# Decayed attention and a gated MLP on one core: the scores of a pair of heads from split q and k in place, on half of the array's rows each

## The chip, the core and the metric

The kernel runs on one NeuronCore of one Trainium2 chip. The core has a matrix engine (TensorE, PE in the profile, with a row of its own, PEld, for its weight loads), three engines for elementwise work (VectorE or DVE, ScalarE or ACT, GpSimd or POOL) and a queue that issues most DMAs (SyncE, SP). Each engine runs its own list of instructions in order, and semaphores make one wait for another. The metric is the device time of one execution in microseconds (us).

## The reference

For 8 batches of 8 heads, with 576 tokens and 64 dimensions per head, and then a gated MLP over the heads side by side (512 columns):

```python
scores = scale * np.matmul(q, k.transpose(0, 1, 3, 2))
log_f = np.log(np.clip(f, 0.0001, 1.0))
cum = np.cumsum(log_f, axis=-1)
decay = cum[:, :, :, None] - cum[:, :, None, :]
scores = np.where(causal, -1000000000.0, scores + decay)
...
attn = attn / (np.sum(attn, axis=-1, keepdims=True) + 1e-09)
return np.matmul(attn, v).astype(np.float32)
...
h = np.maximum(x @ w_in, 0.0)
u, v = (h[..., :d_ff // 2], h[..., d_ff // 2:])
...
v_s = np.einsum('ts,bsd->btd', w_spatial, v_n) + b_spatial[None, :, None]
gated = u * v_s
return (gated @ w_out).astype(np.float32)
```

All of it is asked for in float32.

## The kernel before, in words

**Numbers.** A float32 operand x is held as two parts: hi, x rounded to the type float32r, and lo, x minus hi. A product is hi times hi plus hi times lo plus lo times hi. `split` (L202) makes hi and lo of q and k for a pair of heads: rows 0 to 63 of the tiles hold the first head's 64 dimensions, rows 64 to 127 the second's; the columns are 640 for q (576 tokens, with a place of its own for the tail of each head) and 576 for k.

**Scores.** The heads go in 32 pairs, four pairs to a batch. A head's scores are computed in four blocks of 128 queries against 128, 256, 384 and 512 keys (`scores`, L254); the last 64 queries of both heads share one tile (`scores_tail`, L280, twice 288 keys). For each head `prep` (L215) assembles two operand tiles by DMA out of `hi` and `lo`: `ta` holds q's hi and lo stacked on 128 partitions, against k's hi twice, so that one product gives hi*hi + lo*hi; `tb` holds q's hi and the rows of the decay (68 partitions), against k's lo and the decay, so that a second product gives the rest. That makes six DMAs per head, all on SP's queue. The decay enters as four more rows of the contraction: -8 against the cumulated log decay in two parts, and the reverse. They are made once for all heads and stand in DRAM as `rows_d`. The first pair (`NQ = 1`) is an exception: one float32 tile per head, `tf`, with 66 partitions. `qkt` (L246) issues the two products of a block into one bank of PSUM, `sc`, of which there are two once the MLP runs (three before that).

A block is then masked and scaled by DVE with the row's minimum (L264), goes through exp on ACT (L266) into the tile `tt`, and is divided by its row sum by POOL (L277). `transposes` (L317) turns it on PE (against `ident`) and ACT and DVE take it out in two parts, `eh` and `el` (L314, L315); `attend` (L350) multiplies by v, into `x0` and `x1`. For the first five pairs (`NF`) that product is in float32, and its last one has the 64 keys of the tail: 64 partitions.

**MLP.** `moe` (L429) does one batch: w_in, gate statistics, the spatial product and w_out, all as three-term products into banks called `ps`.

**Order.** `attention` and `moe` are generators that yield an estimate of PE's time after each step; the loop at the end (L566) calls them alternately, so that attention runs a quarter of a batch ahead. That gives each instruction its place in the program; the framework's scheduler then sets the final order on each engine by a simulated timeline, in which an instruction whose operands or bank are not ready is passed by others. So neighbours in the code need not be neighbours on PE. With weights loaded ahead, about the first five pairs run without the MLP beside them.

Of the kernel before, what the change touches and what calls it, by code (L numbers as in the profile page):

```python
# [19 lines left out]
NF = 5            # pairs of heads whose attention times v is in float32  # L20
NQ = 1            # pairs of heads whose scores are in float32
# [17 lines left out]
def attn_gmlp_kernel(ctx: ExitStack, tc: tile.TileContext, qk, v, f, w_in, w_sp, b_sp, w_out, out):  # L39
    """Decayed causal attention, then a gated MLP with a spatial gate.  # L40

    A float32 operand x of a matrix product is held as two float32r parts, hi = x rounded to
    float32r and lo = x - hi, and a product is hi*hi + hi*lo + lo*hi, summed in float32.
    """
# [30 lines left out]
    # ---- decay rows of the score products: [-8 | c_hi], [-8 | c_lo], [c_hi | 8], [c_lo | 8],  # L75
    # the queries' columns as in qk, then the keys'; c = cumulated log decay; [-8 | c], [c | 8] in float32 ----
# [3 lines left out]
    def decay_consts(r, rows):  # L80
        r = f32(r)
        G.memset(r[:, 0:rows, 0:640], -8.0)
        G.memset(r[:, rows:2 * rows, 640:QK], 8.0)
        for p0, h in ((0, 0), (32, 1)):
            V.memset(r[p0:p0 + 32, :, S - 64 * h:640 - 64 * h], 0.0)

    def queries_rows(r, rows, copy, copy_tail):
        r_ = f32(r)
        copy(r[:, rows:2 * rows, 0:TL], r_[:, 0:rows, 640:640 + TL])
        for p0, h in ((0, 0), (32, 1)):  # L90
            copy_tail(r[p0:p0 + 32, rows:2 * rows, TL + 64 * h:S + 64 * h], r_[p0:p0 + 32, 0:rows, 640 + TL:QK])

    def decay_rows():
# [4 lines left out]
        r0 = cst.tile([64, 2, QK], F32, name="r0", tag="el")  # L98
        decay_consts(r0[:], 1)
# [3 lines left out]
        V.tensor_tensor_scan(out=r0[:, 0, 640:QK], data0=ones, data1=ft, initial=0.0, op0=ALU.mult, op1=ALU.add)  # L103
        queries_rows(r0[:], 1, V.tensor_copy, A.copy)
        return r0

    def split_rows(ws, r0):
        rt = ws.tile([64, 4, QK], F32R, name="rt", bufs=1)
        decay_consts(rt[:], 2)
        A.copy(rt[:, 0, 640:QK], r0[:, 0, 640:QK])  # L110
        G.tensor_tensor(out=rt[:, 1, 640:QK], in0=r0[:, 0, 640:QK], in1=f32(rt[:, 0, 640:QK]), op=ALU.subtract)
        queries_rows(rt[:], 2, A.copy, A.copy)
        SY.dma_start(out=rows_d[:], in_=f32(rt[:]))
# [21 lines left out]
    def load64(src, dh, dl, raw, w, a, mark=None):  # L135
        """A block of a float64 weight, read as two 32-bit words: round to float32 and split."""
# [16 lines left out]
    def load_first(ws):  # L153
        """What the first steps of the MLP need: w_in for the gate's half, the spatial weights."""
# [26 lines left out]
    def load_rest(n, w_v, dh, dl, tag, bufs):  # L181
        """An eighth of a weight, by way of tiles that the MLP doesn't use yet."""
# [17 lines left out]
    vts, tab, parts, r0s = {}, {}, {}, []  # L200

    def split(P):  # L202
        """q and k of a pair of heads, one head on each half of the partitions, split."""
        if P < NQ:
            return
        raw = wk.tile([128, QK], F32, name="raw", tag="raw")
        SY.dma_start(out=raw, in_=qk[P])
# [3 lines left out]
        for c in (slice(0, 640), slice(640, QK)):  # L211
            G.tensor_tensor(out=lo[:, c], in0=raw[:, c], in1=f32(hi[:, c]), op=ALU.subtract)  # L212
        parts[P] = (f32(hi[:]), f32(lo[:]))

    def prep(P, h):  # L215
        """The operands of a head's scores: ta = [q_hi; q_lo | k_hi; k_hi], tb = [q_hi; decay | k_lo; decay]."""
        p = slice(64 * h, 64 * h + 64)
        if P < NQ:
            ta = wk.tile([66, QK], F32, name="tf", tag="ta", bufs=2)
            SY.dma_start(out=ta[0:64, :], in_=qk[P, p, :])  # L220
            last['dma', P, h] = SY.dma_start(out=ta[64:66, :], in_=r0s[0][32 * h + P:32 * h + P + 1])
            tab[P, h] = (ta,)
            return
        hi, lo = parts[P]
        ta = wk.tile([128, QK], F32R, name="ta", tag="ta", bufs=2)
        tb = wk.tile([128, QK], F32R, name="tb", tag="tb", bufs=2)
# [6 lines left out]
        tab[P, h] = (ta, tb)  # L233
# [12 lines left out]
    def qkt(o, P, h, q0, k0, n, first, final):  # L246
        """Scores of 128 queries against n keys."""
        k0 += 640
        ts = tab[P, h]
        for t in ts:  # L250
            r = 66 if len(ts) == 1 else 128 if t is ts[0] else 68
            mm(o, t[0:r, q0:q0 + 128], t[0:r, k0:k0 + n], first and t is ts[0], final and t is ts[-1])

    def scores(P, h):  # L254
        """Masked scores of a head, negated and scaled; row maxima; exp; row sums; normalised."""
        nm = wk.tile([128, 4], F32, name="nm", tag="nm", bufs=3)
        sm = wk.tile([128, 4], F32, name="sm", tag="sm", bufs=3)
        for i in range(NB):
            n = 128 * (i + 1)
            q0 = 128 * i  # L260
            sc = PS['s'].tile([128, 512], F32, name="sc")
            qkt(sc[:, 0:n], P, h, q0, 0, n, True, True)
            t = tt[h][:, TOFF[i]:TOFF[i] + n]
            V.tensor_tensor_reduce(out=t, in0=sc[:, 0:n], in1=zm[:, 640 - n:640], scale=-0.125, scalar=3.0e38,  # L264
                                   op0=ALU.add, op1=ALU.min, accum_out=nm[:, i:i + 1])
            last["exp", P, h, i] = A.activation(t, t, AF.Exp, bias=nm[:, i:i + 1], scale=-1.0,  # L266
                                                accum_out=sm[:, i:i + 1])
            yield 2 * max(107, 0.42 * n)
        V.tensor_scalar(out=sm, in0=sm, scalar1=1.0e-9, scalar2=None, op0=ALU.add)
        V.reciprocal(sm, sm)  # L270
        for i in range(NB):
            n = 128 * (i + 1)
            t = tt[h][:, TOFF[i]:TOFF[i] + n]
            if i == 3 and P < PPB:
                A.activation(t, t, AF.Copy, scale=sm[:, i:i + 1])
            else:
                G.tensor_scalar(out=t, in0=t, scalar1=sm[:, i:i + 1], scalar2=1.0, op0=ALU.mult, op1=ALU.mult)  # L277
        yield 0

    def scores_tail(P):  # L280
        nm = wk.tile([128, 4], F32, name="nm", tag="nm", bufs=3)
        sm = wk.tile([128, 4], F32, name="sm", tag="sm", bufs=3)
# [98 lines left out]
    def attention(b, ws=None):  # L381
        for P in range(b * PPB, (b + 1) * PPB):
            if P == 0:
                r0s.append(decay_rows())
                for h in range(2):
                    prep(0, h)
# [231 lines left out]
```

## Time and profile before

| what | value |
|---|---|
| time, median of 3 runs | 834.18 us (832.36 to 836.0) |
| profiled execution, first to last instruction (span) | 827.5 us |
| matmul busy (PE) | 791.4 us, 4968 instructions |
| weight loads busy (PEld) | 711.3 us |
| DVE, ACT, POOL busy | 608.6, 535.9, 464.7 us |
| moved by DMA | 109.16 MB |

The page has no other time of the profiled execution than its span; the median of the runs is 6.7 us longer. In the page a share is of the span, and matmuls are pipelined, so that the durations of neighbours overlap and a PE that is always busy is not thereby at its best. A row of a group gives its count, its busy time, the mean duration of one, and then the idle time just before it with what ended that. A row of a timeline gives the start, the length, engine, line, what is written and read, partitions x columns of the weights (64*128), and partitions x columns of the moving operand. Where several instructions merge into one row, only the first one's shape is shown.

### The profile page before, as it was taken

The numbers are of one execution on the slowest core, as the hardware profiler recorded it, in microseconds if no ns is written. First come the engines' busy times: TensorE is split into PE (matmuls) and PEld (weight loads), VectorE is DVE, ScalarE is ACT, GpSimd is POOL, SyncE is SP. The second block draws the span as 40 slices with busy tenths as digits, with TensorE's granted clock in tenths as the row PEclk, the third lists the DMA queues.
The fourth block names the chain that finished last, engine by engine and source line by source line (L and its number), as shares of the span: only waits on it lengthen the run. The fifth ranks groups of instructions, "written<-read, shape, count | busy, mean of one in ns | idle before, by whom it ended". The sixth has DMA issues, their size and how long they took to land.

```text
span 827.5 us, 15557 instructions
## 1 busy us (share of the span) xinstructions
PE 791.4 (96%) x4968; PEld 711.3 (86%) x4968; DVE 608.6 (74%) x1830; ACT 535.9 (65%) x1383; POOL 464.7 (56%) x631
## 2 busy tenths in 40 slices
PE   7889898999999999999999999999999999999997
PEld 4667687879889998999899988898899988999896
DVE  5776998987788777787677776768776777776431
ACT  5888556765777657767677666666676657665331
POOL 5674788664585555555575555465664547543131
PEclk7799987999999999999999999999999999999999
DMA  8997747446653664556455564546535664430001
GB/s 234 209 260 194 192 134 183 106 109 164 165 137 96 141 170 118 128 111 165 129 129 139 139 137 117 130 105 157 150 78 124 165 154 117 109 77 13 27 1 64
DMA packets 49851, 109.16 MB, mean 132 GB/s; under 512 B 7405, under 2 KB 15597, under 8 KB 49706
## 3 DMA queue, kind: packets, MB, share of 16 engines
q1 hardware_dynamic: 49450, 107.64, 52.2%
q8 instruction: 40, 0.66, 0.3%
q10 hardware_dynamic: 320, 0.52, 0.2%
q14 instruction: 41, 0.34, 0.1%
HBM read 39.53 MB, written 10.68 MB: 61 GB/s over the span
## 4 chain that ended last, share of the span: by engine, by line
PE 71%; DVE 4%; DMA 1%; ACT 1%; POOL 1%; issue 1%; SPq 0%; ACTq 0%; POOLq 0%; DVEq 0%
PE ps L198 40%; PE sc L198 12%; PE x L198 9%; PE tp L325 6%; PE tp L198 2%; PE tp L338 2%; DMA out_dram<-o 1%; DVE vx L461 1%; DVE el L315 1%; POOL tt L277 1%; DVE xh L416 0%; ACT eh L314 0%; ACT o L534 0%; POOL mv L460 0%; DVE tt L264 0%
## 5 line engine op out<-in xcount | busy, mean ns | idle before, releaser
L277 POOL TENSOR_SCALAR tt<-tt,sm 128x128 f32<-128x128 f32 (+2 forms) x248 | 131.5, 548 | 110.8 <-DVE sm L270 91.0
L264 DVE CUSTOM_DVE_ANT_0 tt<-sc,zm 128x128 f32<-128x128 f32 (+3 forms) x256 | 122.5, 486 | 69.0 <-PE tp L325 44.5
L266 ACT ACTIVATE tt<-tt,nm 128x128 f32<-128x128 f32 (+3 forms) x256 | 144.1, 564 | 41.0 <-DVE nm L264 37.1
L314 ACT CAST eh<-tp 128x512 fp32r<-128x512 f32 (+1 forms) x270 | 110.8, 424 | 58.8 <-PE tp L325 42.0
L315 DVE TENSOR_TENSOR el<-tp,eh 128x512 fp32r<-128x512 f32 (+1 forms) x270 | 127.2, 484 | 14.7 <-ACT eh L314 11.1
L198 PE MATMUL sc<-ta 128*128 128x128 f32 (+1 forms) x372 | 122.8, 340 | 13.6 <-DVE nm L264 9.0
L198 PE MATMUL sc<-tb 68*128 68x128 f32 (+1 forms) x372 | 117.9, 325 | 2.2 <-DMA tb<-lo 1.7
L325 PE MATMUL tp<-ident,tt 128*128 128x128 f32 x640 | 115.4, 284 | 2.0 <-DVE el L315 1.1
L212 POOL TENSOR_TENSOR lo<-raw,hi 128x640 fp32r<-128x640 f32 (+1 forms) x62 | 92.3, 1509 | 21.1 <-ACT hi L210 20.9
L198 PE MATMUL x<-eh,vt 128*128 128x320 f32 (+4 forms) x378 | 102.5, 287 | 1.3 <-DVE eh L347 0.9
L510 POOL TENSOR_TENSOR gl<-u,gh 128x256 fp32r<-128x256 f32 (+1 forms) x64 | 51.8, 810 | 84.9 <-ACT gh L509 79.0
L198 PEld LDWEIGHTS sc<-ta 128*128 128x128 f32 x372 | 72.3, 196 | 22.3 <-DVE nm L264 15.9
L198 PE MATMUL x<-el,vt 128*128 128x256 f32 x324 | 91.2, 307 | 0.3 <-DVE el L315 0.3
L325 PEld LDWEIGHTS tp<-ident,tt 128*128 128x128 f32 x640 | 78.7, 143 | 13.5 <-POOL tt L277 2.6
L198 PEld LDWEIGHTS sc<-tb 68*128 68x128 f32 x372 | 72.3, 196 | 5.7 <-issue 2.7
L198 PE MATMUL ps<-sph,vnh 128*128 128x256 f32 (+1 forms) x240 | 73.4, 306 | 2.7 <-DVE u L506 1.6
L198 PEld LDWEIGHTS x<-eh,vt 128*128 128x128 f32 x378 | 71.4, 190 | 5.0 <-DVE eh L347 1.1
L198 PE MATMUL ps<-xh,winh 128*128 128x256 f32 (+1 forms) x232 | 71.1, 307 | 0.8 <-ACT u L484 0.6
L198 PE MATMUL ps<-sph,vnl 128*128 128x256 f32 (+1 forms) x240 | 71.6, 298 | 0.0
L198 PE MATMUL ps<-spl,vnh 128*128 128x256 f32 (+1 forms) x240 | 71.6, 298 | 0.0
L374 DVE TENSOR_TENSOR xl<-x,xh 64x256 fp32r<-64x256 f32 (+1 forms) x128 | 57.4, 452 | 18.5 <-ACT xh L373 16.1
L373 ACT CAST xh<-x 64x256 fp32r<-64x256 f32 (+1 forms) x128 | 49.6, 393 | 32.2 <-PE x L198 30.3
(192 smaller groups left out, 2128.9 us busy)
## 6 DMA issues: line engine op xcount, KB each, us to landing
raw<-in_dram SPq DMA_DIRECT2D x31, 608.0 KB
ta<-hi SPq DMA_DIRECT2D x62, 304.0 KB
vraw<-in_dram SPq DMA_DIRECT2D x32, 320.0 KB
tb<-hi SPq DMA_DIRECT2D x62, 160.0 KB
ta<-lo SPq DMA_DIRECT2D x62, 160.0 KB
tb<-lo SPq DMA_DIRECT2D x62, 144.0 KB
ta<-hi SPq DMA_DIRECT2D x62, 144.0 KB
out_dram<-o SPq DMA_DIRECT2D x32, 256.0 KB
```

The lines of the kernel that those rows point to most:

```text
L198: T.matmul(o, l, r, start=st, stop=sp)
L212: G.tensor_tensor(out=lo[:, c], in0=raw[:, c], in1=f32(hi[:, c]), op=ALU.subtract)
L264: V.tensor_tensor_reduce(out=t, in0=sc[:, 0:n], in1=zm[:, 640 - n:640], scale=-0.125, scalar=3.0e38, op0=ALU.add, op1=ALU.min, accum_out=n ...
L266: last["exp", P, h, i] = A.activation(t, t, AF.Exp, bias=nm[:, i:i + 1], scale=-1.0, accum_out=sm[:, i:i + 1])
L277: G.tensor_scalar(out=t, in0=t, scalar1=sm[:, i:i + 1], scalar2=1.0, op0=ALU.mult, op1=ALU.mult)
L314: A.copy(h_ap, ps)
L315: V.tensor_tensor(out=l_ap, in0=ps, in1=f32(h_ap), op=ALU.subtract)
L325: T.transpose(out=tp[:, (i - c) * 128:(i - c + 1) * 128], in_=tt[h][:, TOFF[i] + 128 * c:TOFF[i] + 128 * c + 128], identity=ident)
L338: T.transpose(out=tp[:, j * 128:(j + 1) * 128], in_=tl[:, c * 128:(c + 1) * 128], identity=ident)
L373: last[P, h] = A.copy(hi, ps[m0:m0 + 64, 0:n])
L374: V.tensor_tensor(out=lo, in0=ps[m0:m0 + 64, 0:n], in1=f32(hi), op=ALU.subtract)
L510: G.tensor_tensor(out=gl[j][:, 0:nt], in0=g, in1=f32(gh[j][:, 0:nt]), op=ALU.subtract)
```

## The change

`prep` assembles nothing any more. The products read `hi` and `lo` where `split` left them: the first head on partitions 0 to 63, the second on 64 to 127, so that each product uses half of the array's rows. A block of scores is now four products per head: hi*hi, lo*hi, hi*lo, and the decay, which has a tile of its own (`dec`, two in turn, 128 partitions, all zero but four rows per head, which `prep` brings in by two DMAs per pair: for the first batch from the tile `rt`, after that from `rows_d`). `scores` does both heads of a pair together: the code names the first product of the first head, the first of the second head, the second of the first head and so on, into two banks. The tail's scores take all 128 partitions, as four products in place of two per head. The first pair goes the same way as the others; `NQ`, `tf` and the float32 rows are gone. `hi`, `lo` have two buffers each. In `attention` both heads' transposes come first, then both heads' scores of the next pair, then the tails, then both products with v. The core of it:

```diff
+    decs = [cst.tile([128, QK], F32R, name=f"dec{i}") for i in range(2)]
...
     def split(P):
-        if P < NQ:
-            return
         raw = wk.tile([128, QK], F32, name="raw", tag="raw")
...
-        hi = wk.tile([128, QK], F32R, name="hi", tag="hi")
-        lo = wk.tile([128, QK], F32R, name="lo", tag="lo")
+        hi = wk.tile([128, QK], F32R, name="hi", tag="hi", bufs=2)
+        lo = wk.tile([128, QK], F32R, name="lo", tag="lo", bufs=2)
...
-        parts[P] = (f32(hi[:]), f32(lo[:]))
+        parts[P] = (hi, lo, decs[P % 2])
...
-    def prep(P, h):
...
-        SY.dma_start(out=f32(ta[0:64, :]), in_=hi[p, :])
-        SY.dma_start(out=f32(ta[64:128, 0:640]), in_=lo[p, 0:640])
-        SY.dma_start(out=f32(ta[64:128, 640:QK]), in_=hi[p, 640:QK])
-        SY.dma_start(out=f32(tb[0:64, 0:640]), in_=hi[p, 0:640])
-        SY.dma_start(out=f32(tb[0:64, 640:QK]), in_=lo[p, 640:QK])
-        SY.dma_start(out=f32(tb[64:68, :]), in_=rows_v[:, P, h, :])
+    def prep(P):
+        d = decs[P % 2]
+        for h in range(2):
+            o = f32(d[64 * h:64 * h + 4, :])
+            if P < PPB:
+                SY.dma_start(out=o, in_=f32(r0s[0][32 * h + P:32 * h + P + 1]))
+            else:
+                SY.dma_start(out=o, in_=rows_v[:, P, h, :])
...
+    TERMS = ((0, 0), (1, 0), (0, 1), (2, 2))
...
-            sc = PS['s'].tile([128, 512], F32, name="sc")
-            qkt(sc[:, 0:n], P, h, q0, 0, n, True, True)
+            sc = [PS['s'].tile([128, 512], F32, name="sc") for h in range(2)]
+            for a, b in TERMS:
+                for h in range(2):
+                    p = slice(64 * h, 64 * h + 64)
+                    mm(sc[h][:, 0:n], parts[P][a][p, q0:q0 + 128], parts[P][b][p, 640:640 + n], a == b == 0, a == 2)
...
-            for h in range(2):
-                qkt(sc[:, 0:288], P, h, 512, k0, 288, h == 0, h == 1)
+            for a, b in TERMS:
+                mm(sc[:, 0:288], parts[P][a][:, 512:640], parts[P][b][:, 640 + k0:928 + k0], a == b == 0, a == 2)
...
             yield from transposes(P, 0)
+            yield from transposes(P, 1)
             if nxt:
-                yield from scores(P + 1, 0)
+                yield from scores(P + 1)
             yield from transposes_tail(P)
...
-            yield from attend(P, 0, xh, xl)
-            yield from transposes(P, 1)
-            if nxt:
-                yield from scores(P + 1, 1)
-            yield from attend(P, 1, xh, xl)
+            for h in range(2):
+                yield from attend(P, h, xh, xl)
```

How the order of instructions changes is shown at three places. The first is on PE, beside the MLP, in the scores of the eleventh pair. Before, this is the first head's block of 384 keys (`sc_2775`) and its block of 512 (`sc_2797`), among products of w_in (`ps_2925`):

```order
L198 MATMUL ps_2925<-winh_86,xh_2248 128x512
L198 MATMUL sc_2775<-ta_2716 128x384
L198 MATMUL sc_2775<-tb_2717 128x384
L198 MATMUL ps_2925<-winl_87,xh_2248 128x512
L198 MATMUL ps_2925<-winh_86,xl_2249 128x512
L198 MATMUL sc_2797<-ta_2716 128x512
L198 MATMUL sc_2797<-tb_2717 128x512
L325 MATMUL tp_2748<-ident_66,tt0_94 128x128 x2
```

Now the block of 512 keys of the same pair: the first head's bank is `sc_2906`, the second head's `sc_2907`; `ps_3428` and `ps_3491` are banks of the spatial product. First the piece with the first head, then, a few products further on, the piece with the second:

```order
L189 MATMUL ps_3428<-spl_93,vnh_2889 128x256
L189 MATMUL ps_3428<-sph_92,vnl_2890 128x256
L189 MATMUL sc_2906<-hi_2661 128x512
L189 MATMUL sc_2906<-hi_2661,lo_2662 128x512
L189 MATMUL sc_2906<-lo_2662,hi_2661 128x512
L189 MATMUL sc_2906<-dec0_86 128x512
L189 MATMUL ps_3428<-sph_92,vnh_2968 128x256
L189 MATMUL ps_3428<-spl_93,vnh_2968 128x256
```

```order
L189 MATMUL ps_3428<-sptb_95,vb_101 128x256
L317 MATMUL tp_2938<-ident_66,tl_98 128x128 x3
L189 MATMUL sc_2907<-hi_2661 128x512
L189 MATMUL sc_2907<-hi_2661,lo_2662 128x512
L189 MATMUL sc_2907<-lo_2662,hi_2661 128x512
L189 MATMUL sc_2907<-dec0_86 128x512
L189 MATMUL ps_3491<-sph_92,vnh_2808 128x256
L189 MATMUL ps_3491<-spl_93,vnh_2808 128x256
```

Two products per head and block have become four, and the two heads, which alternate in the code, stand apart: four of one head, other work on the whole array, four of the other.

The second place is on PE early in the program, where the second pair's scores run without the MLP. Before, the second head's blocks of 128 to 512 keys (`sc_401` to `sc_416`) stand among transposes (`tp`) and products with v (`x1_356`):

```order
L198 MATMUL sc_401<-ta_251 128x128
L198 MATMUL sc_401<-tb_252 128x128
L198 MATMUL x1_356<-ef_98,vraw_241 128x320 x3
L325 MATMUL tp_387<-ident_66,tt1_95 128x128 x3
L198 MATMUL sc_406<-ta_251 128x256
L198 MATMUL sc_406<-tb_252 128x256
L198 MATMUL sc_411<-ta_251 128x384
L198 MATMUL sc_411<-tb_252 128x384
L198 MATMUL sc_416<-ta_251 128x512
L198 MATMUL sc_416<-tb_252 128x512
```

Now the second head's block of 256 keys (`sc_340`) and the first head's block of 384 (`sc_353`):

```order
L304 MATMUL tp_296<-ident_66,tt0_96 128x128 x2
L189 MATMUL sc_340<-hi_244 128x256
L189 MATMUL sc_340<-hi_244,lo_245 128x256
L189 MATMUL sc_340<-lo_245,hi_244 128x256
L189 MATMUL sc_340<-dec1_87 128x256
L189 MATMUL sc_353<-hi_244 128x384
L189 MATMUL sc_353<-hi_244,lo_245 128x384
L189 MATMUL sc_353<-lo_245,hi_244 128x384
L189 MATMUL sc_353<-dec1_87 128x384
L304 MATMUL tp_300<-ident_66,tt0_96 128x128
L189 MATMUL x0_443<-ef_100,vraw_268 128x256
L304 MATMUL tp_303<-ident_66,tt1_97 128x128 x4
```

Here two heads do meet, where the second head's four end and the first head's next four begin.

The third place is on SP's queue, for the fifth pair. Before, its twelve DMAs, the two heads' mixed by the scheduler:

```order
L232 DMA tb_821<-rows_d_85 4x1216
L227 DMA ta_820<-hi_715 64x1216
L229 DMA ta_820<-hi_715 64x576
L230 DMA tb_821<-hi_715 64x640
L228 DMA ta_820<-lo_716 64x640
L227 DMA ta_828<-hi_715 64x1216
L231 DMA tb_821<-lo_716 64x576
L228 DMA ta_828<-lo_716 64x640
L229 DMA ta_828<-hi_715 64x576
L230 DMA tb_829<-hi_715 64x640
L231 DMA tb_829<-lo_716 64x576
L232 DMA tb_829<-rows_d_85 4x1216
```

Now, two small ones (`dec0`) among the loads of q and k (`raw`), v (`vraw`) and the MLP's weights:

```order
L196 DMA raw_793<-in_0_dram 128x1216
L154 DMA wraw_814<-in_4_dram 128x576
L215 DMA vraw_483<-in_1_dram 128x640
L160 DMA wraw_867<-in_4_dram 64x576 x2
L211 DMA dec0_86<-rows_d_85 4x1216 x2
L165 DMA br_872<-in_5_dram 1x576
```

What stood on SP between two loads is gone but for these two.

More of the change, by code (lines that the diff above doesn't have):

```diff
@@ L20 @@
 NF = 5
-NQ = 1
 LEAD = 0.25
@@ L78, in attn_gmlp_kernel, with decay_rows @@
     rows_v = rows_d[:].rearrange("(h n) r s -> r n h s", h=2)
[L80 to L93, printed above, removed]
+    decs = [cst.tile([128, QK], F32R, name=f"dec{i}") for i in range(2)]
+    def decay_rows(ws):
         ft = wk.tile([64, S], F32, name="ft", tag="vt")
@@ L97, in decay_rows @@
         V.memset(ones, 1.0)
-        r0 = cst.tile([64, 2, QK], F32, name="r0", tag="el")
-        decay_consts(r0[:], 1)
+        rt = ws.tile([64, 4, QK], F32R, name="rt", bufs=1)
+        r = f32(rt[:])
+        G.memset(r[:, 0:2, 0:640], -8.0)
+        G.memset(r[:, 2:4, 640:QK], 8.0)
+        for p0, h in ((0, 0), (32, 1)):
+            V.memset(r[p0:p0 + 32, :, S - 64 * h:640 - 64 * h], 0.0)
         V.tensor_scalar(out=ft, in0=ft, scalar1=1.0e-4, scalar2=1.0, op0=ALU.max, op1=ALU.min)
@@ L102, in decay_rows @@
         A.activation(lnc[0:1, 2:3], ft[0:1, 0:1], AF.Exp)
[L103 to L113, printed above, removed]
+        c = wk.tile([64, S], F32, name="c", tag="xl", bufs=5)
+        V.tensor_tensor_scan(out=c, data0=ones, data1=ft, initial=0.0, op0=ALU.mult, op1=ALU.add)
+        A.copy(rt[:, 0, 640:QK], c)
+        V.tensor_tensor(out=rt[:, 1, 640:QK], in0=c, in1=f32(rt[:, 0, 640:QK]), op=ALU.subtract)
+        V.tensor_copy(rt[:, 2:4, 0:TL], r[:, 0:2, 640:640 + TL])
+        for p0, h in ((0, 0), (32, 1)):
+            A.copy(rt[p0:p0 + 32, 2:4, TL + 64 * h:S + 64 * h], r[p0:p0 + 32, 0:2, 640 + TL:QK])
+        for d in decs:
+            G.memset(f32(d[:]), 0.0)
+        r0s.append(rt)
     last = {}
@@ L244, in prep_v, with scores @@
         vts[P] = vt
[L246 to L257, printed above, removed]
+    TERMS = ((0, 0), (1, 0), (0, 1), (2, 2))
+    def scores(P):
+        nm = [wk.tile([128, 4], F32, name="nm", tag="nm", bufs=4) for h in range(2)]
+        sm = [wk.tile([128, 4], F32, name="sm", tag="sm", bufs=4) for h in range(2)]
         for i in range(NB):
@@ L268, in scores @@
[L268 to L277, printed above, removed]
+            sc = [PS['s'].tile([128, 512], F32, name="sc") for h in range(2)]
@@ new lines, in scores @@
+            for a, b in TERMS:
[3 more added lines that the diff above has]
+            for h in range(2):
+                t = tt[h][:, TOFF[i]:TOFF[i] + n]
+                V.tensor_tensor_reduce(out=t, in0=sc[h][:, 0:n], in1=zm[:, 640 - n:640], scale=-0.125,
+                                       scalar=3.0e38, op0=ALU.add, op1=ALU.min, accum_out=nm[h][:, i:i + 1])
+                last["exp", P, h, i] = A.activation(t, t, AF.Exp, bias=nm[h][:, i:i + 1], scale=-1.0,
+                                                    accum_out=sm[h][:, i:i + 1])
@@ new lines, in scores @@
+            yield 4 * max(107, 0.45 * n)
+        for h in range(2):
+            V.tensor_scalar(out=sm[h], in0=sm[h], scalar1=1.0e-9, scalar2=None, op0=ALU.add)
+            V.reciprocal(sm[h], sm[h])
+            for i in range(NB):
+                n = 128 * (i + 1)
+                t = tt[h][:, TOFF[i]:TOFF[i] + n]
+                if i == 3 and P < PPB:
+                    A.activation(t, t, AF.Copy, scale=sm[h][:, i:i + 1])
+                else:
+                    G.tensor_scalar(out=t, in0=t, scalar1=sm[h][:, i:i + 1], scalar2=1.0, op0=ALU.mult, op1=ALU.mult)
@@ L383, in attention @@
             if P == 0:
-                r0s.append(decay_rows())
-                for h in range(2):
-                    prep(0, h)
+                split(0)
+                decay_rows(ws)
+                prep(0)
                 warm = ps_a.tile([128, 512], F32, name="x0")
@@ L390, in attention @@
                     mm(warm, zm[:, 0:128], zm[:, 0:512], True, True)
-                split_rows(ws, r0s[0])
+                yield from scores(0)
                 split(1)
-                yield from scores(0, 0)
                 yield from scores_tail(0)
-                yield from scores(0, 1)
             nxt = P + 1 < NPAIR
@@ L398, in attention @@
             if nxt:
-                prep(P + 1, 0)
-                prep(P + 1, 1)
+                prep(P + 1)
+            if P == 1:
+                SY.dma_start(out=rows_d[:], in_=f32(r0s[0][:]))
             yield from transposes(P, 0)
+            yield from transposes(P, 1)
             if nxt:
-                yield from scores(P + 1, 0)
+                yield from scores(P + 1)
             yield from transposes_tail(P)
@@ L410, in attention @@
             xl = wk.tile([128, S], F32R, name="xl", tag="xl", bufs=5)
-            yield from attend(P, 0, xh, xl)
-            yield from transposes(P, 1)
-            if nxt:
-                yield from scores(P + 1, 1)
-            yield from attend(P, 1, xh, xl)
+            for h in range(2):
+                yield from attend(P, h, xh, xl)
             V.tensor_copy(xh[:, S:640], f32(xl[:, TL:S]))
```

28 lines of the change are left out of this document (6 added, 22 removed).

## The prediction, made before the changed kernel had run

> **What bounds the kernel now.** The page comes first: its busy shares, its slices, its chain.
>
> ```profile
> PE 791.4 (96%) x4968; PEld 711.3 (86%) x4968; DVE 608.6 (74%) x1830; ACT 535.9 (65%) x1383; POOL 464.7 (56%) x631
> ...
> PEclk7799987999999999999999999999999999999999
> DMA  8997747446653664556455564546535664430001
> ...
> PE 71%; DVE 4%; DMA 1%; ACT 1%; POOL 1%; issue 1%; SPq 0%; ACTq 0%; POOLq 0%; DVEq 0%
> PE ps L198 40%; PE sc L198 12%; PE x L198 9%; PE tp L325 6%; PE tp L198 2%; PE tp L338 2%; DMA out_dram<-o 1%; DVE vx L461 1%; DVE el L315 1%; POOL tt L277 1%; DVE xh L416 0%; ACT eh L314 0%; ACT o L534 0%; POOL mv L460 0%; DVE tt L264 0%
> ```
>
> TensorE (PE) is busy for 96% of the span and carries 71% of the chain that ended last. A busy PE need not be a PE at its peak, so the stages are looked at next (PE's busy time, the granted clock, the DMA share), and then what PE waits for.
>
> ```profile
> 0.00:140.00 140.00, 120.77 (x538) 0.85 0.77 198
> 140.00:780.00 640.00, 628.15 (x4167) 1.00 0.51 125
> ...
> PE sc L198 <- DVE nm L264: 9.0, 11, 1.9
> ...
> PE sc L198 <- DMA ta<-hi: 1.8, 2, 1.4
> ...
> PE sc L198 <- DMA tb<-lo: 1.7, 2, 1.4
> ```
>
> For 640 us PE has no gap worth naming (628.15 busy); in the first 140 us it stands idle for 19.2. The operands that the change no longer moves by DMA are waited for twice for 1.8 us and twice for 1.7 us in the whole run. So what a product costs on PE comes straight into the time, and what a DMA costs hardly does. The forecast is therefore a count of PE's instructions times their distance in time.
>
> **Products: the distances now.** In the timeline of PE the column to read is the start: a product's cost is the distance to the next start, since the durations overlap. Two places between 200 and 290 us hold all four widths:
>
> ```profile
> 208.12 0.34 PE L198 MATMUL sc<-ta 128*128 128x384 f32 x1
> 208.30 0.34 PE L198 MATMUL sc<-tb 68*128 68x384 f32 x1
> 208.48 0.40 PE L198 MATMUL sc<-ta 128*128 128x512 f32 x1
> 208.71 0.39 PE L198 MATMUL sc<-tb 68*128 68x512 f32 x1
> 208.94 0.28 PE L325 MATMUL tp<-ident,tt 128*128 128x128 f32 x1
> ...
> 284.20 0.23 PE L198 MATMUL sc<-ta 128*128 128x128 f32 x1
> 284.27 0.28 PE L198 MATMUL sc<-tb 68*128 68x128 f32 x1
> 284.38 0.36 PE L198 MATMUL x<-eh,vt 128*128 128x320 f32 x1
> 284.58 0.28 PE L198 MATMUL sc<-ta 128*128 128x256 f32 x1
> 284.69 0.28 PE L198 MATMUL sc<-tb 68*128 68x256 f32 x1
> 284.81 0.31 PE L198 MATMUL x<-el,vt 128*128 128x320 f32 x1
> ...
> 284.21 0.19 PEld L198 LDWEIGHTS sc<-tb 68*128 68x128 f32 x1
> 284.32 0.19 PEld L198 LDWEIGHTS x<-eh,vt 128*128 128x128 f32 x1
> 284.43 0.19 PEld L198 LDWEIGHTS sc<-ta 128*128 128x128 f32 x1
> ```
>
> 512 columns take 0.23 us, 384 take 0.18, 256 take 0.12, and two of 128 take 0.18 together (0.09 each). The rows of 68 partitions cost what those of 128 cost: it is the columns that count. Around a product of 128 columns the weight loads (PEld) start 0.11 us apart, and no closer; so a run of several products of 128 columns goes at 0.11 each.
>
> **What the change does to them.** Before, a block of scores of one head is two products, of 128 and of 68 partitions. Now it is four of 64 partitions. For a pair, the two by two blocks of each width were 4 products and are 8. If no two run at the same time, a pair goes from 4 x (0.09 + 0.12 + 0.18 + 0.23) = 2.5 us to 8 x (0.11 + 0.12 + 0.18 + 0.23) = 5.1 us: 2.6 us more, and over 31 pairs 81 us. (The tail's scores are 8 products of 288 columns before and after, now all of the full 128 partitions: nothing.)
>
> The code writes the two heads alternately, and a head on partitions 0 to 63 uses other rows of the array than one on 64 to 127, so two products could run side by side and the 81 us would be nothing. But the order of instructions, above, shows that the scheduler does not keep the alternation. At the first place a head's four products stand together, with other work before the other head's; at the second two heads meet, but only end to start. Counted over PE's whole order: 1,024 half-array score products, and ten half-array products that were there before, stand in 268 unbroken groups, mostly four products of one head (187 groups); neighbours of different heads occur 40 times, most of them where one head's four end and the other's begin. Each such place can save at most about one product of 0.2 us, 8 us in all; I take 3.
>
> **What a change between whole and half array costs.** This the trace of before does show, at ten places: the last product of each early attention (L365, 64 keys) is the only one with 64 partitions. First the group of its weight loads, then PE around one of the ten, then the weight loads there:
>
> ```profile
> L198 PEld LDWEIGHTS x<-ef,vraw 64*128 64x128 f32 x20 | 3.0, 185 | 2.2 <-issue 2.2
> ...
> 62.98 0.58 PE L198 MATMUL x<-ef,vraw 128*128 128x192 f32 x2
> 63.24 0.43 PE L198 MATMUL x<-ef,vraw 64*128 64x64 f32 x2
> 63.60 0.40 PE L198 MATMUL sc<-ta 128*128 128x288 f32 x1
> 63.84 0.30 PE L198 MATMUL sc<-tb 68*128 68x288 f32 x1
> 63.97 0.30 PE L198 MATMUL sc<-ta 128*128 128x288 f32 x1
> ...
> 62.82 0.19 PEld L198 LDWEIGHTS x<-ef,vraw 128*128 128x128 f32 x1
> 63.23 0.29 PEld L198 LDWEIGHTS x<-ef,vraw 64*128 64x128 f32 x2 [0.23 <-issue]
> 63.59 0.19 PEld L198 LDWEIGHTS sc<-ta 128*128 128x128 f32 x1
> 63.70 0.19 PEld L198 LDWEIGHTS sc<-tb 68*128 68x128 f32 x1
> ```
>
> Weight loads normally start as the product before them starts: that for the 62.98 product at 62.82, 0.16 ahead. The first with 64 partitions comes only 0.25 us after 62.98, idle for 0.23, waiting for nothing the profile names ("issue"); the group's row says the same of all ten. From 62.98 to 63.84 it takes 0.86 us. At undisturbed distances it would be 0.16 (192 columns), twice a third of that, 0.11, for 64 columns, and 0.135 for 288: 0.40. Of the 0.46 too much, 0.05 is the second short product's wait for its weight load (0.11 against 0.05 us of columns), which products of 128 columns and more do not have. So going to half the array and back costs 0.40 us: PE runs empty and the next weight load stands open, once each way. Before, PE does this 10 times, now 268: 258 x 0.40 = 103 us. Bounds: 0.22 (only the idle time of the weight loads) gives 57 us, all 0.46 gives 119.
>
> **What goes, and what is hidden.** The twelve DMAs per pair that assembled ta and tb go from SP's queue, with two small ones for the decay in their place. Of waits that is the 1.8 and 1.7 us above and some smaller ones, 4 us. A longer PE also uses up waits for others, most of all in the first 140 us, where PE is idle for 19.2: I take 12 off, bounds 0 and 19. DVE, ACT and POOL have practically the same instructions as before, and stand at 74% or less of a span that grows, so none becomes the bound.
>
> Two waits are new or worse. Both heads of a block now ask for the two score banks at once, and a group's first product holds all of PE's queue until DVE (L264) has emptied its bank; today that wait is 9.0 us in 11 places. The order puts other products between two groups in most of the run, which covers DVE's step; in the first pairs there is little to put there, but what is lost there is within the 19.2 us of idle time. Bounds: 5 us less to 9 more, taken as nothing. And the fourth product of each group reads the decay rows, which two DMAs bring in a whole pair ahead; if that cover failed it would be one wait of DMA length per pair, like the 1.8 us above, 55 us in all, but nothing on SP's queue stands in their way now. I take nothing.
>
> The first pair went in float32 products: 24 of them, from 9.77 us on, in 12.4 us;
>
> ```profile
> 9.77 12.41 PE L198 MATMUL sc<-tf 66*128 66x128 f32 x24 [2.38 <-DMA tf<-r]
> ```
>
> now it has 32 half-array products and 8 tail products, its first load brings in both heads at once, and a copy and two subtractions come between that load and the products. With the clock at 7 tenths there, I take this as even, give or take 5 us.
>
> **Sum.** 81 + 103 - 3 - 4 - 12 = 165 us. The profiled span is 827.5 us, so its successor's is about 992; the median of the runs, 834.2, is 6.7 above the span, and with the same distance the forecast is 999 us.
>
> **Rivals.** (a) The cost of the mode change is smaller. The ten places are float32 products and two instructions long; if leaving the half array costs nothing and only the 0.22 us count, it is 46 us less: 953. If the cost is the float32 products' own and does not occur at all with float32r: 896. Against it: full-array float32 products just before the ten show no such gap. Chances 0.13 and 0.06.
>
> (b) In a half-array run the next weights cannot load while a product of the same rows runs. Then three of each four products pay for the load: 0.11 each, 0.05 for those of 128 columns (already paced by the loads), (3 x 0.05 + 9 x 0.11) = 1.1 us per head, 62 heads, 71 us more: 1070. The rows at 284.21 to 284.43 show loads under running products of the same rows at full array; of the half array only the two loads after 63.23 speak, and they are too short to decide. The Trainium skill states this rule for all of TensorE ("TensorE: Matmul & The Clock Gate", part 3, what overlaps: weight loads overlap with running products only when the row group differs). The full-array rows here disagree with it. Chance 0.11.
>
> (c) The halves run side by side after all: the time falls. This needs neighbours of different heads on PE and no price for the mode change; then eight half products take the time of four whole ones (those of 128 columns 0.11 in place of 0.09, 2 us over the run), the DMA waits go, pair 0 comes to its better end, and it is 834 + 2 - 4 - 5 = 827. It decides from the point at which most of the 1,024 products have the other head's as neighbour; the order shows 40. The Trainium skill has the rule that would carry it ("TensorE: Matmul & The Clock Gate", part 3: products on different row groups start some 4 ns apart and run together); no row of this trace can show it, since nothing in it puts two halves side by side. Chance 0.04.
>
> (d) More idle time lowers the clock: the slices with idle PE at the start stand at 7 tenths. If the first 140 us went at 0.75 in place of 0.85, their 121 us of PE would grow by some 16 us, inside the range. It is no case of its own.
>
> **Numbers.** The forecast, 999 us, has chance 0.66; its own range, from the bounds of its terms other than the mode change (side by side 0 to 8, waits 0 to 19, banks -5 to 9, pair 0 and the clock) and 0.46 at the top of the mode change, is 975 to 1045. To take in (a)'s first case with its own spread, and (b) up to its price, the range is 930 to 1070; left out are the free mode change, (c) and the upper half of (b), under 0.2 together. A difference under 0.5% (4 us) can't be told from none. Faster 0.03 and within 0.5% 0.01 (both case c, the second with a small remainder), slower 0.96 (all the others).
>
> **What would show it right or wrong.** In the profile after: products sc<-hi of 64 partitions, two groups of starts per block, at 0.23 us for 512 columns within a group of four; an idle weight load of about 0.2 us marked "issue" on entering each group, and as much lost on leaving it; a PE chain share of 75% or more; waits on DMA for scores near nothing. If starts of the two heads' products fall together, (c) is right; if 512 columns go at 0.34, (b); if the gap is absent, (a). The forecast is wrong if the span stays under 930.

## The result and the profile after

The changed kernel takes 955.75 us (954.97 to 956.58, 4 runs), the kernel before 834.22 (4 runs): a ratio of 1.146, with a 95% interval of 1.143 to 1.149. It is slower by 121.5 us, where the forecast said 165 (999 us, range 930 to 1070, and 975 to 1045 for the forecast's own mechanism). The profiled execution has a span of 954.4 us.

From the page of the changed kernel, the same rows as before the change:

```profile
PE 930.3 (97%) x5480; PEld 770.6 (81%) x5480; DVE 626.1 (66%) x1830; ACT 544.8 (57%) x1382; POOL 468.1 (49%) x631
...
DMA  6244221110112110112110121111101112001001
...
PE 84%; DVE 3%; POOL 1%; ACT 0%; issue 0%; DVEq 0%; ACTq 0%
PE ps L189 42%; PE sc L189 22%; PE x L189 9%; PE tp L304 7%; PE tp L317 2%; PE tp L189 2%; POOL tt L256 1%; DVE w L136 1%; DVE wa L135 1%; DVE tt L242 0%; DVE wa L133 0%; DVE st L433 0%; DVE xl L353 0%; DVE wa L139 0%; DVE wa L138 0%
```

PE's part of the chain went from 71% to 84%, and that of the score products (sc) from 12% to 22% of a longer span: 102 us before, 211 now. DMA has all but left the slices. PE's busy time grew by 139 us, its idle time fell by 12. The time came where the forecast looked for it, on PE in the score products.

The next lines are the timelines of PE and of its weight loads in the changed kernel, at a block of 512 keys of one head (start, length, engine, line, what it is, count; in brackets the idle time just before, with its releaser):

```profile
303.60 0.55 PE L317 MATMUL tp<-ident,tl 128*128 128x128 f32 x3
304.08 0.50 PE L189 MATMUL sc<-hi 64*128 64x512 f32 x1
304.42 0.40 PE L189 MATMUL sc<-hi,lo 64*128 64x512 f32 x1
304.66 0.39 PE L189 MATMUL sc<-lo,hi 64*128 64x512 f32 x1
304.89 0.39 PE L189 MATMUL sc<-dec 64*128 64x512 f32 x1
305.21 0.42 PE L189 MATMUL ps<-sph,vnh 128*128 128x320 f32 x1
305.47 0.31 PE L189 MATMUL ps<-spl,vnh 128*128 128x320 f32 x1
...
304.07 0.18 PEld L189 LDWEIGHTS sc<-hi 64*128 64x128 f32 x1 [0.17 <-issue]
304.18 0.19 PEld L189 LDWEIGHTS sc<-hi,lo 64*128 64x128 f32 x1
304.42 0.18 PEld L189 LDWEIGHTS sc<-lo,hi 64*128 64x128 f32 x1
304.66 0.18 PEld L189 LDWEIGHTS sc<-dec 64*128 64x128 f32 x1
305.21 0.19 PEld L189 LDWEIGHTS ps<-sph,vnh 128*128 128x128 f32 x1 [0.37 <-issue]
305.32 0.19 PEld L189 LDWEIGHTS ps<-spl,vnh 128*128 128x128 f32 x1
```

This is what the prediction drew from ten short float32 products, now with long float32r ones. Inside the group the distances are 0.23 to 0.24 us, those of 512 columns at full array, and each weight load starts while the product before it streams. The first product carries its own weight load (0.11 more, 304.08 to 304.42). At the far end, the last product began at 304.89 and should have been done 0.23 later; the next load comes at 305.21, and the product after it, of 320 columns, takes 0.26 to the next start in place of 0.15. From the idle time before 304.07 to there, some 0.4 us are lost around one group. Over all 187 groups that hold the four products of one head and nothing else, the loss worked out from the starts in this way is 0.41 us in the median (0.39 to 0.43, depending on the distances taken as undisturbed).

One thing is not what the prediction said. The next rows are from the second place that the section on the change shows, where the order of instructions has the second head's four products of 256 keys and then the first head's four of 384, with nothing between:

```profile
34.01 0.71 PE L189 MATMUL sc<-hi 64*128 64x256 f32 x2
34.40 0.65 PE L189 MATMUL sc<-hi,lo 64*128 64x256 f32 x2
34.61 0.41 PE L189 MATMUL sc<-lo,hi 64*128 64x256 f32 x1
34.82 0.41 PE L189 MATMUL sc<-dec 64*128 64x256 f32 x1
34.85 0.52 PE L189 MATMUL sc<-lo,hi 64*128 64x384 f32 x1
35.17 0.52 PE L189 MATMUL sc<-dec 64*128 64x384 f32 x1
```

The first two rows each hold one product of either block (a merged row shows the shape of the first). So the products of 384 keys began with those of 256, although they come after all four of them in the order of instructions. Beside the MLP, where two blocks of 512 keys meet, it looks like this:

```profile
643.18 0.51 PE L189 MATMUL sc<-hi 64*128 64x512 f32 x2
643.52 0.40 PE L189 MATMUL sc<-hi,lo 64*128 64x512 f32 x2
643.75 0.39 PE L189 MATMUL sc<-lo,hi 64*128 64x512 f32 x2
643.98 0.40 PE L189 MATMUL sc<-dec 64*128 64x512 f32 x2
644.31 0.77 PE L317 MATMUL tp<-ident,tl 128*128 128x128 f32 x5
```

"x2" stands at each: the two heads' products start together (within 0.02 us), and eight take the time of four. The second head's first product did not wait for the first head's last. There are eight groups in which all eight products of two blocks of the same width do this; each saves four distances, 0.7 us at 384 keys and 0.9 at 512, and not the 0.2 that the prediction allowed. In some more groups, as in the rows from 34.01, blocks of different widths overlap and save less.

### The profile page after: what moved, and what is told of

Read it like the earlier page. It is cut to its first block, busy times and chain, and to the rows that moved or that the text cites. A ratio compares the mean times of both kernels' runs of the same rounds, so it can differ in the third digit from the quotient of the medians.

```text
span 954.4 us, 15876 instructions
## 1 busy us (share of the span) xinstructions
PE 930.3 (97%) x5480; PEld 770.6 (81%) x5480; DVE 626.1 (66%) x1830; ACT 544.8 (57%) x1382; POOL 468.1 (49%) x631
## 4 chain that ended last, share of the span: by engine, by line
PE 84%; DVE 3%; POOL 1%; ACT 0%; issue 0%; DVEq 0%; ACTq 0%
PE ps L189 42%; PE sc L189 22%; PE x L189 9%; PE tp L304 7%; PE tp L317 2%; PE tp L189 2%; POOL tt L256 1%; DVE w L136 1%; DVE wa L135 1%; DVE tt L242 0%; DVE wa L133 0%; DVE st L433 0%; DVE xl L353 0%; DVE wa L139 0%; DVE wa L138 0%
## 5 line engine op out<-in xcount | busy, mean ns | idle before, releaser
L201 POOL TENSOR_TENSOR lo<-raw,hi 128x640 fp32r<-128x640 f32 (+1 forms) x63 | 95.0, 1534 | 73.5 <-ACT hi L199 66.4
L189 PE MATMUL sc<-hi 64*128 64x128 f32 (+4 forms) x320 | 120.9, 400 | 6.8 <-DVE nm L242 6.3
L189 PE MATMUL sc<-dec 64*128 64x128 f32 (+4 forms) x320 | 100.6, 326 | 3.9 <-DMA dec<-rt 3.9
L189 PEld LDWEIGHTS sc<-hi 64*128 64x128 f32 (+1 forms) x320 | 57.5, 188 | 56.4 <-issue 22.3
L189 PE MATMUL sc<-hi,lo 64*128 64x128 f32 (+4 forms) x320 | 98.9, 325 | 2.8 <-POOL lo L201 2.8
L189 PE MATMUL sc<-lo,hi 64*128 64x128 f32 (+4 forms) x320 | 99.6, 324 | 0.0
L304 PEld LDWEIGHTS tp<-ident,tt 128*128 128x128 f32 x640 | 76.7, 142 | 19.6 <-issue 9.3
L353 DVE TENSOR_TENSOR xl<-x,xh 64x320 fp32r<-64x320 f32 (+1 forms) x128 | 58.0, 453 | 52.0 <-ACT xh L352 49.9
L189 PE MATMUL x<-el,vt 128*128 128x256 f32 (+2 forms) x324 | 86.2, 297 | 0.1
L352 ACT CAST xh<-x 64x320 fp32r<-64x320 f32 (+1 forms) x128 | 50.3, 393 | 48.4 <-PE x L189 46.7
L189 PE MATMUL ps<-xh,winh 128*128 128x256 f32 (+1 forms) x232 | 73.4, 316 | 0.5 <-ACT vx L432 0.5
```

What stands on the lines that cost most here:

```text
L189: T.matmul(o, l, r, start=st, stop=sp)
L201: (V if P == 0 and n else G).tensor_tensor(out=lo[:, c], in0=raw[:, c], in1=f32(hi[:, c]), op=ALU.subtract)
L304: T.transpose(out=tp[:, (i - c) * 128:(i - c + 1) * 128], in_=tt[h][:, TOFF[i] + 128 * c:TOFF[i] + 128 * c + 128], identity=ident)
L352: last[P, h] = A.copy(hi, ps[m0:m0 + 64, 0:n])
L353: V.tensor_tensor(out=lo, in0=ps[m0:m0 + 64, 0:n], in1=f32(hi), op=ALU.subtract)
```

## Experiments

The first question was which of the two terms, twice the products or the changes of mode, made the time, and whether the new order of the steps had a part in it. `full_array_four` takes away the changes of mode alone, `half_array_two` half of the products alone, `full_array_two` both; `pair_of_banks` keeps everything and lets the halves meet.

**full_array_four.**

```diff
-                    p = slice(64 * h, 64 * h + 64)
+                    p = slice(0, 128)
```

> The changed kernel with the same four products per head and block, but each on all 128 partitions of hi, lo and dec (so each head's scores are the sum of both heads': the computation is changed in that). The number of products, their columns and the order of the code stay; the changes between half and whole array go (268 groups to the 10 of the early attention). My theory, 0.41 us per round trip: 955.8 - 258 x 0.41 = 850, plus some 9 us for the places where two halves ran side by side, so 860, range 845 to 875. Rival 1, the mode change costs nothing and the added time is the products alone: 955 or more. Rival 2, the added time is the new order (both heads' banks at once): also 940 to 955.

It took 881.5 us (ratio 1.058, 1.054 to 1.062): 74 us less than the changed kernel. Rivals 1 and 2 fall: most of the added time hangs on the halves of the array, since products, columns and the order of the code are the same. It is 21 us more than I said, and outside my range.

**half_array_two.**

```diff
-            for a, b in TERMS:
+            for a, b in (TERMS[0], TERMS[3]):
```

> The changed kernel with only the products hi*hi and decay per head and block, each on its half of the array (hi*lo and lo*hi are left out of the four blocks: the scores are less exact). Half as many products, nearly as many groups (231 in place of 268). My theory: half of the products' distances, 4 x 0.64 us per pair over 31 pairs, less what was side by side: -75, and 37 groups fewer: -15; 955.8 - 90 = 866, range 850 to 885. Rival 1, products all run side by side anyhow and only the mode change costs: 955.8 - 15 = 940. Rival 2, the new order: 940 to 955.

879.0 us (ratio 1.055, 1.051 to 1.060), in the range: half of the products, and the 37 groups that went with them, were worth 77 us.

**full_array_two.** Both edits.

> Both at once: two products per head and block, on all 128 partitions (hi*lo and lo*hi left out, both heads summed). PE then has the work of the kernel before in the blocks, in the order of the changed kernel and without the operand DMAs. My theory: nothing of the added time is left, and the waits for operand DMAs and some of the idle time at the start go: 834 less 5 to 30, so 805 to 829, I say 818. Rival 2, the new order and its banks cost the time: well over 850.

825.6 us (ratio 0.991, 0.988 to 0.994), as expected. With PE's old amount of work in the blocks nothing of the added time is left, in the changed kernel's order. But the two edits do not add up evenly: from two to four products on the full array costs 55.9 us (825.6 to 881.5), on half of it 76.7 (879.0 to 955.8). PE's distances say 74 to 82 for both. Part of the difference is not the products: on the half array 37 more groups come with them, some 12 us at the 0.33 us per group that is measured further on.

**full_array_six** and **before_doubled** ask where the rest went.

```diff
-            for a, b in TERMS:
+            for a, b in TERMS[:3] + TERMS[1:3] + TERMS[3:]:
```

> full_array_four with lo*hi and hi*lo issued twice: six products per head and block on all 128 partitions (the scores are changed by that). Going from two products to four added 56 us where the distances say 74 to 82; my theory is that PE's first extra time falls partly on small waits, and that these are nearly used up with four. Then the next two cost nearly their full distances: 881 + 75 = 956, range 945 to 965. Rival, a product simply costs less than its distance says (0.7 of it): 881 + 56 = 937.

957.1 us (ratio 1.148, 1.143 to 1.153), in the range, and the rival's 937 falls. The next two products cost 75.7 us, where the first two had cost 55.9: the product has its full distance, and what the first ones lacked fell on time in which PE had been waiting anyway.

In the kernel before, each product of a block twice:

```diff
+            twice = 2 if len(ts) == 2 and n != 288 else 1
+            for c in range(twice):
...
```

> The kernel before with each of the two products of a block issued twice (pairs 2 to 32, not the tails; the scores are changed by that): the changed kernel's number of products, all on the whole array, in the old order and with the operand DMAs. Distances: 31 pairs x 4 x (0.10 + 0.12 + 0.18 + 0.23) = 78 us. My theory, that a good quarter of the first added PE time falls on small waits: 834 + 55 = 889, range 880 to 900. Rival, all of it lands in the time, as the forecast took it but for 16 us: 834 + 78 = 912, or 896 with those 16.

883.8 us against 834.4 for the kernel before, measured beside it (ratio 1.060, 1.052 to 1.067), in the range: 49 us for 78 us of distances, in the old order and with the old DMAs. So this slack was in the kernel before, and it was more than the 16 us that the forecast took off.

**one_half_alone.** The same order and groups as the changed kernel, but nothing that can run side by side:

```diff
-                    p = slice(64 * h, 64 * h + 64)
+                    p = slice(0, 64)
```

> The changed kernel, but both heads' products on partitions 0 to 63 (so both heads' scores are the first head's): the same code, order and groups, and nothing that could run side by side. My theory: in the changed kernel some 14 groups hold both heads' four products and save about 0.7 us each, and the first pair runs side by side too; so 955.8 + 10 + 5 = 971, range 962 to 980. Rival, halves never run side by side: 956.

965.9 us (ratio 1.158, 1.150 to 1.166), in the range: 10 us more than the changed kernel, so side by side saves 10 there. Against full_array_four (881.5) this kernel differs by the mode alone: 84 us for 258 more round trips (from the whole array to the half and back), 0.33 each.

**pair_of_banks.** One tile of two banks for both heads (and for the tail), so that both are free at the same moment:

```diff
-            sc = [PS['s'].tile([128, 512], F32, name="sc") for h in range(2)]
+            sc2 = PS['s'].tile([128, 2, 512], F32, name="sc")
+            sc = [sc2[:, h, :] for h in range(2)]
...
```

There is one such tile at a time. Beside the MLP that is the same two banks as before; ahead of it there were three banks and are now two, and where the last batch of the MLP borrows a bank of the scores it takes both.

> The changed kernel, whole computation, with one tile of two banks for both heads of a block in place of two tiles of one bank, so that both heads' banks come free together: then the order on PE is really alternating (118 of 138 groups are the eight products of a block, heads in turn). My theory with halves that run side by side: a block takes four distances (2.6 us per pair, as before the change) and 128 more round trips than before at 0.41: 834 + 3 + 52 less 15 to 30 of waits, so 860 to 875, I say 868; waits for the one pair of banks may add up to 20. Rival, halves don't run side by side: only the fewer groups count: 955.8 - 130 x 0.41 = 902 or more.

898.1 us (ratio 1.077, 1.074 to 1.081): better than the changed kernel by 58 us, but 30 worse than I said and outside my range, and by its time alone hardly to be told from the rival's 902. Its timeline tells them apart. PE around one block:

```profile
303.47 0.31 PE L189 MATMUL x<-eh,vt 128*128 128x320 f32 x1
303.71 0.50 PE L189 MATMUL sc<-hi 64*128 64x512 f32 x2
304.05 0.39 PE L189 MATMUL sc<-hi,lo 64*128 64x512 f32 x2
304.28 0.40 PE L189 MATMUL sc<-lo,hi 64*128 64x512 f32 x2
304.52 0.39 PE L189 MATMUL sc<-dec 64*128 64x512 f32 x2
304.84 0.50 PE L189 MATMUL ps<-woh,gl 128*128 128x512 f32 x1
```

All eight products stand in four distances. What I had too small is the price of the banks; what PE waits for in this kernel begins with

```profile
PE sc L189 <- DVE nm L243: 18.2, 12, 5.7
PE tp L306 <- DVE el L296: 6.1, 7, 1.0
PE ps L189 <- ACT o L512: 6.0, 7, 1.6
```

against 6.3 us for the first of these in the changed kernel. Two controls with the same banks separate the two: the same code with both heads on partitions 0 to 63, and with all 128 partitions.

**pair_of_banks_one_half.**

```diff
-                    p = slice(64 * h, 64 * h + 64)
+                    p = slice(0, 64)
```

> pair_of_banks with both heads' products on partitions 0 to 63 (both heads' scores are the first head's): the same order and groups as pair_of_banks, eight products each, without side by side. My theory: four more distances per block, 2.5 us per pair, 79 us, less what falls on waits (62 us in that kernel): 945 to 975, I say 960. Rival, side by side gains nothing there: 898.

959.8 us (ratio 1.151, 1.143 to 1.159), as expected. Side by side is worth 62 us here: the rival falls.

**pair_of_banks_full.**

```diff
-                    p = slice(64 * h, 64 * h + 64)
+                    p = slice(0, 128)
```

> pair_of_banks with every product on all 128 partitions (both heads summed): no mode change, nothing side by side, and one pair of banks for both heads. It shows what the single pair of banks costs, beside full_array_four (881) with two single banks, and by pair_of_banks_one_half (960) what 128 mode changes cost. My theory: 128 x 0.41 = 52 less what falls on waits, so 960 - 45 = 915, and the banks then cost about 30. Rival, the mode change costs less than half of that in this form: 935 or more.

919.4 us (ratio 1.106, 1.103 to 1.109), 4 us from what I said; the rival's 935 falls. The single pair of banks costs 38 us beside full_array_four (881.5); 11 of them are lost before the first product of the MLP, which starts at 107.2 us here and at 96.0 there. The 128 more round trips cost 40 us (959.8 - 919.4), 0.32 each, as in the changed kernel with twice as many.

**before_new_order.** Does the new order by itself do anything?

```diff
             yield from transposes(P, 0)
+            yield from transposes(P, 1)
             if nxt:
                 yield from scores(P + 1, 0)
+                yield from scores(P + 1, 1)
...
             yield from attend(P, 0, xh, xl)
-            yield from transposes(P, 1)
-            if nxt:
-                yield from scores(P + 1, 1)
             yield from attend(P, 1, xh, xl)
```

> The kernel before, whole computation, with nothing changed but the order of the steps in attention: both heads' transposes, then both heads' scores of the next pair, then the tail, then both products with v, as in the changed kernel. full_array_two, which has this order, the old PE work and no operand DMAs, took 825.6. My theory: order and DMAs hardly matter beside PE's work, so 834 give or take 6. Rival, the new order costs: 845 or more. If it comes out at 826, the gain of full_array_two was the order's, and there is a kernel better than both.

860.9 us against 831.0 for the kernel before, measured beside it (ratio 1.036, 1.033 to 1.038): my theory is wrong here and the rival right. These are the first of PE's waits in this kernel, and then the longest of SP's own:

```profile
PE x L198 <- DMA vraw<-in_dram: 6.2, 4, 2.7
PE ps L198 <- ACT o L533: 6.1, 5, 2.0
PE sc L198 <- DMA tb<-rows_d: 5.6, 5, 1.5
PE sc L198 <- DVE nm L264: 5.4, 9, 1.6
PE sc L198 <- DMA ta<-hi: 5.3, 8, 1.7
...
SPq L227 <- PE sc L198: 178.0, 29, 10.3
```

With both heads' scores in one stretch, the two buffers of ta and of tb are held until the end of it; the DMA that assembles the next pair's (L227) stands on SP's queue for up to 10.3 us until PE is done with them, and I take it that the load of v behind it comes late for that reason. The kernel before has the same wait, but shorter: 107.4 us in all, 6.6 at most. Added up over all rows, PE is idle for DMAs for 24 us here and for 7 in the kernel before; that accounts for 17 of the 30 us, and the rest is not traced to a cause. In the changed kernel those DMAs do not exist, and full_array_two, with this order, takes 826. So the operand DMAs, which the prediction put at 4 us in the old order, would be worth up to some 35 in the new one (the two kernels also differ in the first pair and in the buffers of hi and lo): without them the new order costs nothing.

No version tried that keeps all the products of the scores is better than the kernel before; the best of them with halves is pair_of_banks, at 1.077.

## Why the prediction was right, and its size too large

**Direction and places.** The forecast counted PE's distances, and PE's distances were it. In medians, the 121.5 us fall into three: the products, 881.5 - 833.5 = 48 (833.5 is the kernel before, measured beside that run); the changes of mode, 965.9 - 881.5 = 84; side by side, 955.8 - 965.9 = -10. The 48 hold all else that changed too: by full_array_two the new order, the missing DMAs and the first pair are worth -8 of them and the products 56.

**Where luck helped.** 955.75 us lies outside 975 to 1045, the range that the prediction gave for its own mechanism. It lies inside 930 to 1070 because the range was opened downwards for rival (a), a smaller price of the mode change. The time comes out 3 us from that rival's 953, but the rival is not what happened: the price in a lone group is the 0.41 us that the forecast used, and what brought the time down was slack on PE. That the stated range held is therefore in part luck.

**The products.** 81 us less 16 of waits were forecast, 48 measured. The distance itself was right (75.7 us for two more products per block where no waits are left). The term that was mis-sized is the waits: "A longer PE also uses up waits for others ... I take 12 off, bounds 0 and 19", with 4 more for the DMAs.

**The changes of mode.** 103 us were forecast, 84 measured. The 0.40 us, read at ten places with short float32 products, is 0.41 at a lone group of four in the changed kernel. Per round trip only 0.33 arrives in the time (0.32 with the pair of banks): I take it that the rest again falls where PE would have waited. Products and mode changes together, 81 + 103, less the 10 of side by side, would be 174 us; 121.5 arrived. So some 50 us were hidden, where I took 16 (12 of idle time and 4 of DMA waits), and the bound of 19 for the idle time did not hold.

**Why the bound failed.** I read PE's waits from its idle time, 19.2 us in the first 140 us and next to nothing after. But a matmul's duration overlaps the next one's, so PE is busy on the page while its starts stand too far apart. Adding up the distances of the 4,179 matmuls that all the full-array kernels share (the MLP, transposes, products with v; not the scores) from the trace shows it: 672 us in the kernel before, 641 in full_array_four, 634 in full_array_six. The same matmuls with the same shapes take 31 us less, and then 8 less. Of the 31, some 10 are gone in full_array_two already (663 us), which has the work of the kernel before on PE; the other 21 go when PE has more in between, and in the old order, too, before_doubled takes 21 less than the kernel before (651). That is the slack. PE's idle time on the page went only from 36 to 32 us between the kernel before and full_array_four. Stretches in which a start comes more than 0.3 us later than its columns explain add up to nearly 50 us before and nearly 30 in full_array_four. How much of the smaller ones is waiting for other engines, and how much weight loads behind short products, the runs do not separate.

**Side by side.** 3 us were forecast, with a bound of 8; it is 10. "Each such place can save at most about one product of 0.2 us" was wrong in kind: the two heads' four and four overlap from the first product on.

**The rivals.** (a), a smaller price of the mode change: no, in a lone group it is 0.41, and the weight load after the group stands idle too (0.37 at 305.21). (b), weights that cannot load while a product of the same rows runs: no. 512 columns go at 0.23 within a group, and the loads at 304.42 and 304.66 start as the product before begins. (c), side by side: the mechanism is real (pair_of_banks, 62 us), but the order grants it at few places, 10 us in all, and even where nearly every block has it, four changes of mode per pair remain, 40 us in the time, and the one pair of banks costs 38 more, so that the half array is slower than before. (d), a lower clock: no; PE's granted clock in the first 140 us is 0.90 (0.85 before).

```profile
0.00:140.00 140.00, 123.84 (x613) 0.90 0.38 116
140.00:911.00 771.00, 768.32 (x4639) 1.00 0.14 44
```

**What was not a term.** Nothing was taken for the new order and the banks. In the changed kernel that stands (full_array_two, 8 us faster than before). But with the operand DMAs the new order costs 30 us (before_new_order), which the prediction did not see: it priced the DMAs in the old order alone. For the DMAs of the decay rows nothing was taken either, and PE waits for them once, for 3.9 us.

## What to carry to other kernels

Look at the order in which the instructions reach TensorE before counting on two half-array products at once: alternation in the code is not alternation on the engine, and where two products get their banks one after the other, a scheduler can take them apart, as it did here; one tile for both banks kept them together, at 38 us for the lost freedom. Each stay on the half array costs its entry and exit, so it must be long. Two halves side by side only bring eight half products back to the time of four, which the whole array with stacked operands had already; there was nothing to pay 0.4 us per group from.

When PE's work grows, do not charge all of it: add up the distances between starts of work that does not change, compare them with the undisturbed distances of the same shapes, and take that slack off first. Here the 4,179 matmuls take 672 us, and would take some 620 by the distances inside undisturbed groups (an estimate from 0.11 us for 128 columns, 0.12 for 256, 0.18 for 384 and 0.23 for 512). That is about the 50 us that were hidden, under a page that said 96% busy.

## What the runs showed of the hardware

- Going from whole to half array and back costs about 0.4 us around one group (no weight load starts until the product before has run out, and then the load stands open): 0.40 read at float32 products of the kernel before, 0.41 at float32r products of the changed one. Of that, 0.32 to 0.33 us per round trip arrived in the time.
- Products on rows 0 to 63 and on 64 to 127 run fully side by side: eight in four distances (rows from 303.71 us of pair_of_banks). It happens also when the order of instructions has four of the one and then four of the other (rows from 34.01 us of the changed kernel), so the second half's products pass the first half's that are still waiting.
- On the half array, weights for the next product load while a product on the same rows runs, as on the whole array (loads at 304.42 and 304.66 us of the changed kernel).
- A half-array product of n columns costs what a whole-array one of n columns does: 0.23 us for 512 (medians in one_half_alone: 0.23 for 512, 0.18 for 384, 0.12 for 256, 0.11 for 128).
